# A decode layer on one core: K and V of the last heads in other pieces, one piece fewer of wo and of w2

## The chip, the core and the metric

The kernel runs on one core of a Trainium2 chip. TensorE (PE) multiplies matrices, with the loads of its weights shown apart (PEld); VectorE (DVE) and ScalarE (ACT) work on rows; GpSimd (POOL) fills and masks; SyncE (SP) issues most of the transfers from the chip's main memory, which run on 16 DMA engines. On-chip data lies in 128 partitions. The metric is the device time of one execution in microseconds; lower is better.

## The reference

One token passes through an attention block and a two-layer network, both conditioned on a vector c:

```python
mod = (_silu(c) @ w_mod).reshape(c.shape[0], 6, 1, -1)      # sa, ca, ga, sb, cb, gb
h = _layernorm(x) * (1 + ca) + sa
x = x + ga * _A_ref(h, k_cache, v_cache, wq, wo)            # attention, then @ wo
h = _layernorm(x) * (1 + cb) + sb
x = x + gb * (relu(h @ w1) @ w2)
```

x and c have 512 values. The attention has 32 query heads of 128 values and 8 heads of K and V; four query heads share one of these. K and V each hold 32,768 positions a head, so that each head has 8.4 MB of K and 8.4 MB of V, in bf16. wo is 4096 x 512 (4.2 MB), w1 512 x 1792 and w2 1792 x 512 (1.8 MB each). Nearly all of the data is K and V, and each byte is read once.

## The kernel before, in words

**Slots and stream.** All large data passes through three slots of 64 KB a partition (the pool `ring`). A slot holds all of one head's K, or its V, or w_mod with wq, or `tail_sb`: wo, w1 and w2. The slots are taken in turn, so K7 goes where V4 was, V6 where K6 was, V7 where V5 was, and the tail where K7 was; a transfer into a slot is issued when the last reader of its former content has finished. The list `stream` gives the order and the pieces of the transfers, and `load` issues them all from SP, which works through them in order: what waits at its head holds up all behind it. A key like `("k", 6, (0, 1))` is one transfer of tiles 0 and 1 of head 6; a head's K or V has four tiles of 64 positions a partition (2.1 MB each). Whoever needs one tile waits for the whole transfer that holds it. c and x are two small transfers issued from ACT, at the start.

**A head.** Each value of K must be transposed before TensorE can use it. `turn_k` does this on VectorE, in place (L441): a transpose a tile, or for the last head a transpose a half tile. `scores` (L460) multiplies the turned K with the queries, 16 products a tile. `softmax` takes the maximum, makes the exponentials P on ScalarE (L497) and transposes P on VectorE (L502). `pv` (L523) multiplies P with V, 16 products a tile. `blocks` and `o_cols` (L552 to L560) divide by the sum and place the head's output as columns of `oT_ps`; `normalise` (L574) and `spread` (L586, L590) bring the outputs of a group of heads, one group for each piece of wo, into the form that wo needs. The order of TensorE's and VectorE's instructions is written out by hand (`manual_schedule`): in a loop over heads, the scores of head g + 1 come before the products of head g with V. The heads from `HALVED` on (V of head 5, K of head 6) are loaded in halves, and the last two heads follow the loop in an order of their own.

**The end.** After the last products with V, `project` multiplies the heads' outputs with the pieces of wo. The first two pieces (six heads) go into rows (L599), which `join_rows` transposes and adds as columns (L617, L622); later pieces go into columns directly (L605), four small products for each of a head's four rows. `keep_clock` (L635) runs products whose result nobody uses. Then come x1T (L740), the second layernorm up to h2T (L307), the products with w1 (L765), relu (L775, L776), the products with w2 (L788: four for each of fourteen blocks, in the pieces of `W2P`), and the last sums (L793, L795).

Of the kernel before, what the change touches and what calls it, by code (L numbers as in the profile page):

```python
# [17 lines left out]
def kernel(  # L18
# [14 lines left out]
    nc = tc.nc  # L33
    P = 128
    _, _, D = A_x.shape
    _, Hkv, Sk, Dh = A_k_cache.shape
# [7 lines left out]
    NTILE = Sk // (P * TK)  # L44
    NG = NTILE // 2

    WOP = [(0, Hkv // 2), (Hkv // 2, Hkv // 4), (Hkv - 2, 1), (Hkv - 1, 1)]
    WOROWS = 2
    LAST = Hkv - 1
    LOOPED = Hkv - 2  # L50
    HALVED = LOOPED - 1
    W2P = [(0, 5), (5, 10), (10, 12), (12, 13), (13, 14)]
    W1P = [(0, KT)]

    OUT0, OUT1 = 30, 34
# [106 lines left out]
    whole, halves = [(0, 1, 2, 3)], [(0, 1), (2, 3)]  # L162
    stream = [("k", 0, halves[0]), ("wm",), ("wq",), ("k", 0, halves[1])]
    for g in range(LOOPED):
        stream += [("k", g + 1, s) for s in (halves if g >= HALVED else whole)] + [("v", g, s) for s in (halves if g >= HALVED else whole)]
    for s in halves:
        stream += [("k", LAST, s), ("v", LOOPED, s)]
    stream += [("v", LAST, (0, 1)), ("v", LAST, (2,)), ("v", LAST, (3,))] + [("wo", i) for i in range(len(WOP))]
    stream += [("w1", i) for i in range(len(W1P))] + [("w2", i) for i in range(len(W2P))]
    pos = [0]  # L170

# [8 lines left out]
    wm_sb = need(("wm",))  # L180
    cx_row = const.tile([16, D // 8], BF16)
    for i, row in enumerate((c[0], A_x[0, 0])):
        nc.scalar.dma_start(out=cx_row[8 * i:8 * i + 8], in_=row.rearrange("(a n) -> a n", a=8))

    ident_bf = const.tile([P, P], BF16)
    make_identity(nc, ident_bf[:])
# [372 lines left out]
    def o_cols(g):  # L559
        nc.tensor.matmul(  # L560
            oT_ps[:, REP * g:REP * (g + 1)], lhsT=Y_tiles.pop(g)[:], rhs=qsel,
            start=True, stop=True, skip_group_check=True,
        )
# [4 lines left out]
    def normalise(g):  # L568

        i = part_of(g)  # L570
        g0, n = WOP[i]
        CH = P // (n * REP)
        if g == g0 + n - 1:
            nc.vector.tensor_tensor(  # L574
                out=oA[i][:], in0=oT_ps[:, REP * g0:REP * (g0 + n)].unsqueeze(2).to_broadcast([P, n * REP, CH]),
                in1=cmask[n * REP][:].unsqueeze(1).to_broadcast([P, n * REP, CH]), op=ALU.mult,
            )
        PT_tiles.pop(g)
# [58 lines left out]
    with tc.manual_schedule(engines={mybir.EngineType.PE, mybir.EngineType.DVE}):  # L637
        build_qbd(0)
        for turn in (turn_k, scores):
            for u in range(NTILE):  # L640
                for half in range(2):
                    turn(0, u, half)
        open_o(0)
        for _ in softmax(0):
            pass
        soft = None
        for g in range(LOOPED):
            h = g + 1
            build_qbd(h)
            for u in range(NTILE):  # L650
                for half in range(2):
                    turn_k(h, u, half)
                    scores(h, u, half)
                if soft and u == 1:
                    next(soft, None)
            if g - 1 in [sum(w) for w in WOP]:
                spread(part_of(g - 2))
            if g >= HALVED:
                pv(g, (0, 1))
            soft = softmax(h)  # L660
            next(soft)
            if g > 0:
                blocks(g - 1)
            next(soft)
            if g > 0:
                o_cols(g - 1)
            next(soft)
            next(soft)
            pv(g, (2, 3) if g >= HALVED else (0, 1, 2, 3))
            if g > 0:  # L670
                normalise(g - 1)
            next(soft)
            open_o(h)
            next(soft)
        g, h = LOOPED, LAST
        build_qbd(h)
        turn_k(h, 0, 0)
        turn_k(h, 0, 1)
        next(soft, None)
        turn_k(h, 1, 0)  # L680
        turn_k(h, 1, 1)
        blocks(g - 1)
        scores(h, 0, 0)
        scores(h, 0, 1)
        scores(h, 1, 0)
        o_cols(g - 1)
        scores(h, 1, 1)
        normalise(g - 1)
        spread(part_of(g - 1))
        bank_max(h, 0)  # L690
        pv(g, (0, 1))
        for u in (2, 3):
            for half in range(2):
                turn_k(h, u, half)
                scores(h, u, half)
        bank_max(h, 1)
        soft = softmax(h)
        next(soft)
        next(soft)
        next(soft)  # L700
        pv(g, (2,), range(6))
        next(soft)
        next(soft)
        open_o(LAST)
        pv(g, (2,), range(6, 16))
        pv(g, (3,))
        next(soft)
        next(soft, None)
        end_b.append(two_banks("end_ps"))
        a_rows.append(row_bank(end_b[0][:, 0, :]))  # L710
        blocks(g)
        pv(LAST, (0, 1))
        o_cols(LAST - 1)
        normalise(LAST - 1)
        pv(LAST, (2,))
        spread(2)
        hid_ps = ps_o.tile([P, 512], F32, tag="o", name="hid_ps")
        nc.vector.memset(hid_ps[:], 0.0)
        pv(LAST, (3,))
        blocks(LAST)  # L720
        hid_st = piece("tail_sb", TAIL + 1280, 32 * FT + 2)
        nc.gpsimd.memset(hid_st, 0.0)
        project(0)
        keep_clock(2)
        o_cols(LAST)
        keep_clock(2)
        project(1)
        normalise(LAST)
        spread(3)
        keep_clock(2)  # L730
        project(2)
        keep_clock(1)
        join_rows()
        keep_clock(1)
        project(3)


        stat2 = const.tile([P, 2], F32)
        x1T = const.tile([P, KT], F32)
        nc.vector.tensor_tensor(out=x1T[:], in0=attnT_ps, in1=modT_sb[:, 2 * KT:3 * KT], op=ALU.mult)  # L740
        nc.vector.scalar_tensor_tensor(
            out=x1T[:], in0=x1T[:], scalar=1.0, in1=xT, op0=ALU.mult, op1=ALU.add, accum_out=stat2[:, 0:1],
        )
        h2T = const.tile([P, KT], BF16)
        x1_ps = []

        def meanwhile():
            e = expand(x1T[:], room("tail_sb", TAIL + 1024, [P, 32, KT]).rearrange("p (m kt) -> p m kt", kt=KT))
            keep_clock(2)
            x1_ps.append(four_rows(e, "x1"))  # L750
            keep_clock(2)

        keep_clock(3)
        layernorm_T(x1T[:], stat2, h2T[:], modT_sb[:, 3 * KT:4 * KT], ncb[:], "ln2", meanwhile)
        x1_rows = const.tile([OUT1, P], F32)
        nc.vector.tensor_copy(out=x1_rows[:], in_=x1_ps[0])
        ffn_ps = end_b[0][0:OUT1, 1, P:2 * P]
        nc.vector.memset(ffn_ps, 0.0)

        NQ = 32 * FT  # L760
        for part, (k0, k1) in enumerate(W1P):
            w1_sb = need(("w1", part))
            for kt in range(k0, k1):
                for q in range(4):
                    nc.tensor.matmul(  # L765
                        hid_ps[32 * q:32 * q + 1, 0:NQ], lhsT=h2T[:, kt:kt + 1],
                        rhs=w1_sb[:, kt - k0, q * NQ:(q + 1) * NQ], start=False, stop=(kt == KT - 1),
                        skip_group_check=True,
                    )
        keep_clock(3)  # L770
        hidT = room("tail_sb", TAIL, [P, 512])[:, 0:NQ].rearrange("p (f e) -> p f e", e=32)
        hid_v = hid_ps[:, 0:NQ].rearrange("p (e f) -> p f e", f=FT)
        hb = hid_st
        for f0, f1 in ((0, FT // 2), (FT // 2, FT)):
            nc.vector.transpose(out=hidT[:, f0:f1], in_=hid_v[:, f0:f1])  # L775
            nc.scalar.activation(  # L776
                out=AP(hb.tensor, hb.offset + 32 * f0 + 31, [hb.ap[0], [32, f1 - f0]]),
                in_=hidT[:, f0:f1, 0], func=ACT.Relu,
            )

        for part, (f0, f1) in enumerate(W2P):
            w2_sb = need(("w2", part))
            for ft in range(f0, f1):
                for i in (0, 2, 1, 3):
                    row = OUT0 + i
                    to, w = (0, 32) if row < 32 else (32, OUT1 - 32)
                    at = 32 * ft + 31 - (row - to)
                    nc.tensor.matmul(  # L788
                        ffn_ps[to:to + w, :], lhsT=hid_st[:, at:at + w], rhs=w2_sb[:, ft - f0, i * P:(i + 1) * P],
                        start=False, stop=(ft == FT - 1 and i % 2 == 1), skip_group_check=True,  # L790
                    )
        o_rows = const.tile([OUT1, P], F32)
        nc.vector.tensor_tensor(out=o_rows[:], in0=ffn_ps, in1=gb_rows[:], op=ALU.mult)  # L793
        o_bf = const.tile([OUT1, P], BF16)
        nc.vector.tensor_tensor(out=o_bf[:], in0=o_rows[:], in1=x1_rows[:], op=ALU.add)  # L795
# [31 lines left out]
```

## Time and profile before

| | us |
|---|---|
| median of 3 runs | 354.38 (354.29 to 354.51) |
| the profiled execution | 354.42 |
| its span, first to last instruction | 352.6 |
| PE busy | 272.3 (77%) |
| DVE busy | 195.6 (55%) |
| ACT busy | 18.7 (5%) |

The mean granted clock of TensorE was 0.926. The core read 149.42 MB from main memory.

In rows of the timeline the first number is the start in us from the start of the span, the second the busy time of the group in us; then engine, line of the code, operation, tiles written and read, shapes and count. In brackets stands how long the engine had been idle before it, and what ended that. An SPq row is the issue of a transfer, not the transfer itself. In rows of the chain of waits, start and duration are followed by what the chain went through. In rows of stretches, the stretch and its length are followed by the busy time and count of PE, PEld, DVE, ACT and POOL, the granted clock, the share of the transfers and GB/s.

### The profile page before, as it was taken

What the parts mean: (1) busy time and instruction counts of PE and PEld (TensorE: products, weight loads), DVE (VectorE), ACT (ScalarE), POOL (GpSimd) and SP (SyncE); (2) the same over time, 40 slices, a digit from 0 to 9 for tenths busy, and PEclk for the clock granted to TensorE, in tenths of its full rate; (3) what the DMA queues carried; (4) which work ended last, traced back from release to release, by engine and by line L of the source; (5) the groups of instructions that cost most, each with busy time, mean ns of one, the idle gap of its engine ahead of it and who ended that gap; (6) DMA issues with size and microseconds to landing.
All of it is one profiled execution on the core that took longest, in us unless ns stands there. A gap on an engine that the chain in (4) does not pass through costs nothing. (4 is left out here: it accounts for less than half of the span.)

```text
span 352.6 us, 3544 instructions
## 1 busy us (share of the span) xinstructions
PE 272.3 (77%) x1310; PEld 111.8 (32%) x1310; DVE 195.6 (55%) x167; ACT 18.7 (5%) x37; POOL 6.0 (2%) x26
## 2 busy tenths in 40 slices
PE   0054980695999679884988499976999999789994
PEld 0021330232333224331333233322444443234442
DVE  7662563983079513965099316956674293743142
ACT  1200003001000010001000100001000100011000
POOL 3000000000000000000000000000000000000000
PEclk9996895698999969998999979996999999999999
DMA  8999989999999999999999999999999999999995
GB/s 353 404 432 456 468 387 461 446 401 446 439 424 440 416 439 446 401 455 446 409 453 446 409 453 431 426 394 439 446 414 427 450 429 424 431 453 398 432 426 213
DMA packets 5222, 149.57 MB, mean 424 GB/s; under 512 B 604, under 2 KB 988, under 8 KB 1628
## 3 DMA queue, kind: packets, MB, share of 16 engines
q1 hardware_dynamic: 5180, 149.43, 98.5%
q8 instruction: 8, 0.13, 0.1%
q14 instruction: 2, 0.02, 0.0%
q10 hardware_dynamic: 32, 0.00, 0.0%
HBM read 149.42 MB, written 0.00 MB: 424 GB/s over the span
## 5 line engine op out<-in xcount | busy, mean ns | idle before, releaser
L441 DVE STREAM_TRANSPOSE Ksb<-Ksb 128x4096 f32<-128x4096 f32 (+1 forms) x34 | 131.5, 3912 | 57.6 <-DMA Ksb<-in_A_k_cache_dram 57.6
L460 PE MATMUL S_ps<-Ksb,qbd 128*128 128x512 bf16 x512 | 118.9, 385 | 19.2 <-DVE Ksb L441 18.3
L523 PE MATMUL o_ps<-Vsb,P_g 128*16 (+1 forms) x512 | 124.3, 401 | 10.9 <-ACT P_g L497 10.0
L460 PEld LDWEIGHTS <-qbd 128*128 128x128 bf16 x512 | 49.2, 97 | 84.9 <-issue 27.6
L523 PEld LDWEIGHTS o_ps<-Vsb,P_g 128*16 x320 | 30.4, 95 | 60.0 <-issue 31.8
L523 PEld LDWEIGHTS <-P_g 128*16 128x16 bf16 x192 | 16.7, 90 | 22.9 <-issue 0.4
L473 DVE TENSOR_REDUCE m_p<-S_ps 128x1 f32<-128x1024 f32 x7 | 8.6, 1223 | 21.8 <-PE S_ps L460 21.8
L502 DVE STREAM_TRANSPOSE P_g<-P_g 128x1024 bf16<-128x1024 bf16 x8 | 10.0, 1245 | 15.6 <-ACT P_g L497 15.6
L494 ACT ACTIVATE nbias<-Mb_ps 128x1 f32<-128x1 f32 x8 | 1.4, 171 | 269.5 <-PE Mb_ps L492 269.5
L324 PE MATMUL mod_ps<-wmq_sb,siluT 128*1 128x512 bf16 x24 | 3.6, 624 | 9.9 <-DMA wmq_sb<-in_w_mod_dram 9.9
L332 DVE STREAM_TRANSPOSE Ksb<-Ksb 128x4096 f32<-128x4096 f32 x2 | 8.8, 4424 | 1.7 <-DMA Ksb<-in_A_k_cache_dram 1.7
L478 PE MATMUL mT_ps<-ident_f,m_p 128*1 128x128 f32 x8 | 2.2, 270 | 8.9 <-DVE m_p L473 7.9
L497 ACT ACTIVATE P_g<-S_ps,nbias 128x1024 bf16<-128x1024 f32 x8 | 8.9, 1114 | 0.2
L560 PE MATMUL acc_ps<-mask_sb,Y 16*128 16x4 f32 x16 | 3.4, 282 | 5.1 <-DVE Y L556 5.1
L552 DVE SCALAR_TENSOR_TENSOR o_ps<-o_ps,Linv,smask 16x512 f32<-16x512 f32 x8 | 5.8, 720 | 2.8 <-PE o_ps L523 2.8
L254 PE MATMUL xc_ps<-cx_sel,wmq_sb 16*128 16x2 bf16 x4 | 0.3, 172 | 8.7 <-DVE wmq_sb L248 8.7
L590 DVE CAST o_sb<-o_ps 128x4 bf16<-128x4 f32 (+2 forms) x4 | 0.7, 167 | 11.1 <-PE o_ps L586 11.1
L415 POOL TENSOR_TENSOR qbd<-qrep_sb,rowpick 128x64 bf16<-128x64 bf16 x8 | 2.4, 299 | 228.0 <-PE S_ps L460 198.3
L509 DVE RECIPROCAL Linv<-L_ps 16x1 f32<-16x1 f32 x8 | 1.0, 126 | 8.3 <-PE L_ps L506 8.3
L556 DVE TENSOR_REDUCE Y<-o_ps 16x128 f32<-16x512 f32 x8 | 5.4, 679 | 0.3
L635 PE MATMUL spare_ps<-qbd,ident_bf 128*128 128x512 bf16 x18 | 5.4, 381 | 0.0
L396 PE MATMUL q_ps<-wmq_sb,hT 128*1 128x512 bf16 x32 | 3.6, 626 | 2.3 <-DMA wmq_sb<-in_A_wq_dram 2.3
(114 smaller groups left out, 71.6 us busy)
## 6 DMA issues: line engine op xcount, KB each, us to landing
Ksb<-in_A_k_cache_dram SPq DMA_DIRECT2D x5, 4096.0 KB, 22.9
Vsb<-in_A_v_cache_dram SPq DMA_DIRECT2D x5, 4096.0 KB, 36.5
wmq_sb<-in_A_wq_dram SPq DMA_DIRECT2D x1, 4096.0 KB, 28.1
Vsb<-in_A_v_cache_dram SPq DMA_DIRECT2D x2, 2048.0 KB, 41.1
Ksb<-in_A_k_cache_dram SPq DMA_DIRECT2D x1, 4032.0 KB, 37.2
wmq_sb<-in_w_mod_dram SPq DMA_DIRECT2D x1, 3072.0 KB, 18.9
tail_sb<-in_A_wo_dram SPq DMA_DIRECT2D x1, 2048.0 KB, 23.2
tail_sb<-in_B_w_dram SPq DMA_DIRECT2D x1, 1792.0 KB, 30.6
```

The costliest lines, as they stand in the source:

```text
L324: nc.tensor.matmul(dst[j // 4][32 * (j % 4):32 * (j % 4) + 1, :], lhsT=src_T[:, kt:kt + 1], rhs=w[:, kt, j * 512:(j + 1) * 512], start=(kt ...
L332: nc.vector.transpose(out=t, in_=t)
L396: nc.tensor.matmul(q_ps[i][32 * a:32 * a + 1, :].rearrange("o (h e) -> o h e", e=32), lhsT=hT[:, kt:kt + 1], rhs=wq_f[:, kt, i, a], start= ...
L441: t = nc.vector.transpose(out=KTt.bitcast(F32), in_=KTt.bitcast(F32))
L460: nc.tensor.matmul(S_ps_tiles[g], lhsT=qbd[g % 2][:, hp, 4 * (7 - s):4 * (7 - s) + P], rhs=KTv[:, 16 * sl:16 * sl + 16, h, :, par], start= ...
L473: behind_loop(nc.vector.reduce_max(out=m_p[:], in_=S_g.rearrange("p g f -> p (g f)"), axis=AX.X))
L497: nc.scalar.activation(out=P_g[:], in_=S_g.rearrange("p g f -> p (g f)"), func=ACT.Exp, bias=nbias[:], scale=scale, accum_out=l_g[:],)
L502: behind_loop(nc.vector.transpose(out=P_g[:], in_=P_g[:]))
L523: nc.tensor.matmul(o_tiles[g][:], lhsT=PT, rhs=Vx, start=first, stop=False, skip_group_check=True)
L552: nc.vector.scalar_tensor_tensor(out=o, in0=o, scalar=Linv_tiles.pop(g)[:], in1=smask[:].unsqueeze(2).to_broadcast([16, 4, Dh]), op0=ALU.m ...
L556: nc.vector.tensor_reduce(out=Y[:], in_=o.rearrange("p s d -> p d s"), op=ALU.add, axis=AX.X)
L635: nc.tensor.matmul(spare[0], lhsT=ident_bf[:], rhs=qbd[0][:, :, 0:P], start=True, stop=True)
```

## The change

- K of head 6 and V of head 5 are each loaded in one transfer instead of two halves.
- At the end of the stream the order was K7a, V6a, K7b, V6b, then V7's tiles 0 and 1, tile 2, tile 3. It is now K7a, K7b, V6a, V6b, V7a, V7b, all halves.
- K7's first half is turned inside the loop's last round, on VectorE ahead of the transpose of head 6's P. The scores of head 7 follow all together, and the products of P of head 6 with V6 come after them.
- wo has three pieces (heads 0 to 3, 4 and 5, 6 and 7) instead of four, so that the outputs of heads 6 and 7 are spread in one step after head 7. `join_rows` now stands ahead of the last piece, followed by six products of `keep_clock`.
- w2 has four pieces of 6, 5, 2 and 1 blocks instead of five of 5, 5, 2, 1 and 1.
- c is loaded in three transfers and x in four, instead of one each.

```diff
-    WOP = [(0, Hkv // 2), (Hkv // 2, Hkv // 4), (Hkv - 2, 1), (Hkv - 1, 1)]
+    WOP = [(0, Hkv // 2), (Hkv // 2, Hkv // 4), (Hkv - 2, 2)]
-    W2P = [(0, 5), (5, 10), (10, 12), (12, 13), (13, 14)]
+    W2P = [(0, 6), (6, 11), (11, 13), (13, 14)]
...
-        stream += [("k", g + 1, s) for s in (halves if g >= HALVED else whole)] + [("v", g, s) for s in (halves if g >= HALVED else whole)]
-    for s in halves:
-        stream += [("k", LAST, s), ("v", LOOPED, s)]
-    stream += [("v", LAST, (0, 1)), ("v", LAST, (2,)), ("v", LAST, (3,))] + [("wo", i) for i in range(len(WOP))]
+        stream += [("k", g + 1, whole[0]), ("v", g, whole[0])]
+    stream += [(x, g, s) for x, g in (("k", LAST), ("v", LOOPED), ("v", LAST)) for s in halves]
+    stream += [("wo", i) for i in range(len(WOP))]
...
-        nc.scalar.dma_start(out=cx_row[8 * i:8 * i + 8], in_=row.rearrange("(a n) -> a n", a=8))
+        for a, n in ((0, 2), (2, 2), (4, 2), (6, 2)) if i else ((0, 3), (3, 3), (6, 2)):
+            nc.scalar.dma_start(
+                out=cx_row[8 * i + a:8 * i + a + n], in_=row.rearrange("(a n) -> a n", a=8)[a:a + n],
+            )
...
+            if h == LOOPED:
+                build_qbd(LAST)
+                for u in (0, 1):
+                    for half in range(2):
+                        turn_k(LAST, u, half)
             next(soft)
             open_o(h)
             next(soft)
...
         o_cols(LAST - 1)
         normalise(LAST - 1)
         pv(LAST, (2,))
-        spread(2)
...
         project(1)
         normalise(LAST)
-        spread(3)
-        keep_clock(2)
+        spread(2)
+        join_rows()
+        keep_clock(6)
         project(2)
-        keep_clock(1)
-        join_rows()
-        keep_clock(1)
-        project(3)
```

Left out above is the written order of head 7's scores and of the products with V6, which is told in the list.

More of the change, by code (lines that the diff above doesn't have):

```diff
@@ L675 @@
         g, h = LOOPED, LAST
-        build_qbd(h)
-        turn_k(h, 0, 0)
-        turn_k(h, 0, 1)
         next(soft, None)
[L680 to L691, printed above, removed]
+        for u in (0, 1):
+            for half in range(2):
+                scores(h, u, half)
         for u in (2, 3):
@@ L695 @@
                 scores(h, u, half)
+        blocks(g - 1)
+        bank_max(h, 0)
         bank_max(h, 1)
@@ L699 @@
         next(soft)
+        o_cols(g - 1)
+        normalise(g - 1)
         next(soft)
-        pv(g, (2,), range(6))
+        spread(part_of(g - 1))
+        pv(g, (0,), range(6))
         next(soft)
@@ L704 @@
         open_o(LAST)
-        pv(g, (2,), range(6, 16))
-        pv(g, (3,))
+        pv(g, (0,), range(6, 16))
+        pv(g, (1,))
         next(soft)
@@ L710 @@
         a_rows.append(row_bank(end_b[0][:, 0, :]))
+        pv(g, (2, 3))
         blocks(g)
```

## The prediction

> **What bounds the kernel now.** I read the page first, its slices of the span and its chain of work, and then the chain of waits in order of time.
>
> ```profile
> DMA  8999989999999999999999999999999999999995
> HBM read 149.42 MB, written 0.00 MB: 424 GB/s over the span
> DMA 19%; PE 5%; DVE 3%; SPq 0%; issue 0%
> ```
>
> ```profile
> 313.20 25.28 DMA tail_sb<-in_A_wo_dram
> 338.50 11.12 DMA tail_sb<-in_B_w_dram
> 349.66 0.29 PE end_ps L788 x4
> ```
>
> The transfers are busy in every slice, and the chain that ends last is transfers from 313 to 349.6 us. The kernel is one uninterrupted stream of 149 MB at 424 GB/s; a half of a K or V (4.19 MB) takes 4.19/0.424 = 9.9 us of it. No byte is removed by the change. So it can move the time in three ways only: a hole in the stream, a cheaper stream, or work after the last bytes that no longer fits behind them. The third needs the timeline of the end, one row per group: start, duration, engine, line, and in brackets the idle time before it.
>
> ```profile
> 321.39 7.07 PE L523 MATMUL o_ps<-Vsb,P_g 128*16 128x512 bf16 x32
> 328.39 0.38 PE L560 MATMUL acc_ps<-mask_sb,Y 16*128 16x4 f32 x2
> 332.36 3.62 PE L523 MATMUL o_ps<-Vsb,P_g 128*16 128x512 bf16 x16
> 336.08 1.03 PE L599 MATMUL end_ps<-tail_sb,o_sb 128*1 128x512 bf16 x16
> 337.05 0.60 PE L635 MATMUL spare_ps<-qbd,ident_bf 128*128 128x512 bf16 x2
> 337.59 0.38 PE L560 MATMUL acc_ps<-mask_sb,Y 16*128 16x4 f32 x2
> 338.52 0.60 PE L599 MATMUL end_ps<-tail_sb,o_sb 128*1 128x512 bf16 x8
> 339.06 0.18 PE L586 MATMUL o_ps<-rsel,oA 128*128 128x4 bf16 x1
> 339.27 0.16 DVE L590 CAST o_sb<-o_ps 128x4 bf16<-128x4 f32 x1 [0.98 <-PE o_ps L586]
> 339.35 0.71 DVE L617 STREAM_TRANSPOSE tail_sb<-end_ps 128x512 f32<-128x512 f32 x1
> 340.60 0.24 PE L622 MATMUL acc_ps<-tail_sb,place 128*32 128x4 f32 x8
> 341.01 0.67 PE L605 MATMUL acc_ps<-o_sb,tail_sb 128*128 128x1 bf16 x16
> 341.71 0.16 DVE L740 TENSOR_TENSOR x1T<-acc_ps,modT_sb 128x4 f32<-128x4 f32 x1 [1.65 <-PE acc_ps L605]
> 343.74 0.22 DVE L307 SCALAR_TENSOR_TENSOR h2T<-cen_ln,rstd_ln,modT_sb 128x4 bf16<-128x4 f32 x1
> 345.33 0.93 PE L765 MATMUL hid_ps<-tail_sb,h2T 128*1 128x448 bf16 x16 [1.28 <-DMA tail_sb<-in_B_w_dram]
> 347.10 0.73 PE L788 MATMUL end_ps<-tail_sb 128*32 128x128 bf16 x20
> 348.30 1.64 PE L788 MATMUL end_ps<-tail_sb 128*32 128x128 bf16 x36 [0.47 <-DMA tail_sb<-in_B_w_dram]
> ```
>
> See two reserves here. h2T is ready at 343.74 + 0.22 = 343.96, but the w1 products start at 345.33, waiting for w1: 1.37 us. The w2 products run from 347.10 to 349.95, 2.85 us; at the pace of their first twenty (0.73 us) 56 would need about 1.75 us, so 1.1 us more is waiting for w2. Together about 2.45 us: a chain of engines that gets later by less costs nothing.
>
> The last V transfer, of one of V7's four tiles, was issued at 287.9 and landed 43.3 us later, at 331.2:
>
> ```profile
> L155 SPq DMA_DIRECT2D Vsb<-in_A_v_cache_dram x1: 433/433/433, 287.9 to 287.9; - x1
> DMA to landing us min/median/max: 43.3/43.3/43.3
> ```
>
> **The change, part by part.**
>
> *K6 and V5 whole; K7, V6, V7 in halves; K7's first half turned ahead of P of head 6.*
>
> ```profile
> 243.99 8.77 DVE L441 STREAM_TRANSPOSE Ksb<-Ksb 128x4096 f32<-128x4096 f32 x2 [1.86 <-DMA Ksb<-in_A_k_cache_dram]
> 257.61 0.33 SPq L155 DMA_DIRECT2D Ksb<-in_A_k_cache_dram  x1
> 257.91 14.08 PE L460 MATMUL S_ps<-Ksb,qbd 128*128 128x512 bf16 x64
> 258.09 8.74 DVE L441 STREAM_TRANSPOSE Ksb<-Ksb 128x4096 f32<-128x4096 f32 x2
> 301.96 8.89 DVE L441 STREAM_TRANSPOSE Ksb<-Ksb 128x2048 f32<-128x2048 f32 x4 [5.83 <-DMA Ksb<-in_A_k_cache_dram]
> 312.83 1.75 SPq L155 DMA_DIRECT2D tail_sb<-in_A_wo_dram  x4
> ```
>
> K6's first half lands at 243.99, so all of K6 9.9 us later, at about 253.8. Its four transposes (8.77 a pair) then end at 253.8 + 17.5 = 271.4 and the last quarter of scores at about 275, where before all scores ended at 257.91 + 14.08 = 272.0. So V6's first half, whose slot is K6's, is issued 3 us later. K7's two halves, now both issued when V4's slot comes free (257.61), lie ahead of it: 19.8 us of stream behind V5, which itself ends near 253.8 + 19.8 = 273.6. Covered by about 18 us. V5's products follow 3 us late and release V7's transfers near 290; the stream then holds K7's rest and V6, to about 311. Covered.
>
> K7's second half landed at 301.96 with V6's first half ahead of it; it now comes 9.9 us earlier, at 292. The turns of K7's first half, four at 2.2 us, hold up P of head 6 from 283 to 292; P is wanted only after the scores of head 7, so nothing waits. Those end near 292 + 1.3 (P's transpose) + 8.9 + 2 = 304.4 instead of 312.8, and wo's issue moves up as much. This gain is worth nothing: V7 fills the stream until 331 either way. Softmax 7 takes until about 307, V6's 64 products (2 x 7.07) until 321.4, and V7's first half runs from there to 328.9 with its small product (0.38), as before.
>
> *V7's second half in one piece.* Here the change costs. Before, tile 2 was multiplied while tile 3 was still coming, and after the last landing only one tile's sixteen products (3.62 us) were left: they ended at 332.36 + 3.62 = 335.98. Now 32 products (7.07 us) must wait for the last byte at 331.2, less a little for fewer pieces: I take 331.15, bounds 330.7 to 331.6. They end at 338.2. TensorE idles 2.3 us before them.
>
> *wo in three, one join later.* Everything from the end of V7's products, E, is one chain. The rows give: first product of wo at E + 0.10; o_cols at E + 1.61; second wo piece at E + 2.46 (it no longer waits for its bytes) to E + 3.06; spread 0.18 and cast 0.16 to E + 3.35; the transpose of the joined rows 0.71 to E + 4.07; the join 0.24, handing on at about E + 4.35; then keep_clock, now six products at 0.22 (two span 0.60, so 0.22 each after the first), which stand ahead of the last wo piece: 1.3, to E + 5.65; that piece, 32 small products where there were two times sixteen (0.67 each, 0.04 a product): 1.2, to E + 6.85. Before, the last piece's sixteen ended at E + 5.70 and were set by wo's landing. So x1T starts at 338.2 + 6.88 = 345.1 instead of 341.71: 3.4 us late, 2.2 from V7 and 1.2 from the order of wo.
>
> *w2 in four.* The last piece is the same fourteenth. h2T is ready at 343.96 + 3.4 = 347.35; w1 has long landed; w2 starts 1.77 later (347.10 - 345.33), at 349.15, with all of w2 there by 349.6, and runs unbroken: 1.75 us, to 350.9. Before it ended at 349.95. At the pace of the last 36 (1.64 us, waits included) 56 would take 2.55 and end at 351.7. I take the first pace, as those twenty waited for nothing.
>
> Sum: 3.4 late, 2.45 of reserve, **+0.95 us**; bounds +0.3 (landing at 330.7, quicker keep_clock) to +1.8. The profiled execution took 354.42 for its span of 352.6, the median is 354.38; I add 0.9 to that: **355.3 us**.
>
> *c and x in seven.* In the compiled program of the changed kernel the extra transfers use up the eight completion semaphores, so SP's w_mod now waits for c's first piece and wq for K0's first half.
>
> ```profile
> 7.99 0.68 DVE L248 TENSOR_TENSOR wmq_sb<-cx_row,pick 16x512 bf16<-16x512 bf16 x1 [1.50 <-DMA cx_row<-in_A_x_dram]
> 12.85 8.77 DVE L332 STREAM_TRANSPOSE Ksb<-Ksb 128x4096 f32<-128x4096 f32 x2 [1.71 <-DMA Ksb<-in_A_k_cache_dram]
> 60.27 13.10 DVE L441 STREAM_TRANSPOSE Ksb<-Ksb 128x4096 f32<-128x4096 f32 x3 [1.86 <-DMA Ksb<-in_A_k_cache_dram]
> 214.85 8.77 DVE L441 STREAM_TRANSPOSE Ksb<-Ksb 128x4096 f32<-128x4096 f32 x2 [10.74 <-DMA Ksb<-in_A_k_cache_dram]
> ```
>
> wq is issued when K0's half has landed, at 12.85; w_mod, 3.1 MB, keeps the stream full some 7 us more, and K0 is in the queue before c is asked for. I cost it at nothing in the stream. c and x themselves, two transfers of 1 KB, were usable at 7.99; seven may come at 8 or, queued one behind another, near 20. At 20 the two turns of K0's half (12.85, 8.77 us), which stand behind c and x on VectorE, and all that follows come 7 to 8 us late; K1's turns, which wait for bytes until 60.27 and have 1.86 us idle, come some 5 us late. By head 5 VectorE waits 10.74 us for K, so this is gone long before the end; without that cover it would be those 5 us.
>
> The Trainium skill (DMA: Bandwidth & Descriptors, on why a DMA increments its semaphore by 16) says that a transfer of two or three rows uses only the two or three lowest-numbered DMA engines; that would favour the late end, and no run so far shows it.
>
> **The rivals.**
>
> *The clock falls in the new gap.* Stretches with TensorE's busy time, and its granted clock third from the right:
>
> ```profile
> 300.60:304.00 3.40, 1.73 (x9) 0.64 (x7) 2.04 (x1) 0.00 (x0) 0.00 (x0) 1.00 1.05 453
> 235.80:239.20 3.40, 0.99 (x5) 0.58 (x4) 2.97 (x5) 0.00 (x0) 0.30 (x1) 0.93 1.03 443
> 239.20:242.60 3.40, 1.38 (x5) 0.57 (x5) 1.54 (x2) 1.38 (x3) 0.00 (x0) 0.50 1.03 443
> 290.00:313.00 23.00, 19.23 (x87) 7.79 (x84) 13.11 (x11) 0.00 (x0) 0.14 (x1) 1.00 1.00 432
> 338.00:349.00 11.00, 9.10 (x129) 4.38 (x129) 3.83 (x19) 0.76 (x3) 0.00 (x0) 1.00 0.97 401
> ```
>
> A stretch with 1.73 of 3.4 us busy kept the clock; one with 0.99 was followed by 0.50. The new gap of 2.3 us leaves 1.1 busy if it falls inside one such stretch, between the two. Half the clock for 3.4 us delays V7's products by 1.7 us: 357.0. The Trainium skill (TensorE: Matmul & The Clock Gate, Part 1) says that the clock is halved after an idle window of about 3.4 us, so 2.3 us would not do it; the row of 235.80 shows that a window need not be wholly idle.
>
> *The end stays with the transfers; faster.* Fewer, larger pieces: the last 11 us ran at 401 GB/s, the large pieces at 432. The 4.4 MB of those 11 us would take 10.2 at the better rate, 0.8 us less: 353.6. It decides only if the engine chain is late by less than 1.65 us at x1T, so that its 2.45 of reserve also covers those 0.8; I have 3.4, of which the seven microseconds of products behind V7's last landing are hard to argue away.
>
> *The parts cancel.* The chain comes out a microsecond shorter than summed, because its pieces overlap more, and the end is set by w2 again: 354.0 to 354.6.
>
> *A hole in the stream at the start*, if w_mod's issue waits for a c that comes late: K0's first half is all there is until about 13, so c at 16 would cost 3 us: 358.
>
> **How the numbers follow.** My forecast 0.55, the clock 0.16, cancelling 0.13, the hole and other stalls 0.07, faster 0.09. A difference of 0.2% (0.7 us) is about what this kernel's measurement tells from none. Of my forecast, +0.3 to +1.8, some 0.4 of the 0.55 lies above 0.7 us: slower 0.63, same 0.28, faster 0.09. The range 354.2 to 357.2 leaves out the faster case and the hole; the forecast's own is 354.7 to 356.2.
>
> **What would show it.** Right: TensorE idle about 2 us until V7's second half lands near 331; 32 products to 338; x1T near 345; w1 and w2 products without waiting for transfers, and the chain of work's last 10 us on engines. Wrong: x1T before 343.5, idle before w2, a clock of 0.5 after 328, or a slice of the transfers under 8 near the start.

## The result and the profile after

| | before | after |
|---|---|---|
| median, run side by side on one chip (22 runs each) | 354.25 us | 354.98 us |
| ratio, 95% interval | | 1.0028 (1.0022 to 1.0034) |
| the profiled execution, its span | 354.42, 352.6 us | 354.87, 353.0 us |
| start of o_rows, the first of the last two sums | 349.98 us | 350.30 us |
| V7's last transfer there for TensorE | 331.2 us | 330.67 us |

The change makes the kernel 0.73 us slower. Single executions, of the kernel before too, now and then took 361 us and more; these are left out everywhere below.

The page of the profile after: TensorE's and VectorE's busy time, the slices of the transfers, the packets, and the chain's shares. Ahead of it stands the one line of the page before that the prediction did not show.

```profile
DMA packets 5222, 149.57 MB, mean 424 GB/s; under 512 B 604, under 2 KB 988, under 8 KB 1628
```

```profile
PE 274.6 (78%) x1311; PEld 113.0 (32%) x1311; DVE 194.0 (55%) x163; ACT 18.7 (5%) x37; POOL 5.8 (2%) x25
...
DMA  8999989999999999999999999999999999999994
...
DMA packets 4501, 149.57 MB, mean 424 GB/s; under 512 B 524, under 2 KB 780, under 8 KB 1164
...
DMA 26%; PE 6%; DVE 5%; issue 0%; ACT 0%; DVEq 0%
```

The transfers are still busy in every slice: no hole. There are 721 packets fewer for the same bytes. The last slice is a 4 where it was a 5: the last packets of the stream end at 348.75, where they ended at 349.30 before, and yet the span is longer. So the work behind the last bytes has become the longer part. The timeline of the end shows it (start, busy time, engine, line, and in brackets the idle time before):

```profile
315.13 13.97 PE L525 MATMUL o_ps<-Vsb,P_g 128*16 128x512 bf16 x64
...
329.04 0.38 PE L562 MATMUL acc_ps<-mask_sb,Y 16*128 16x4 f32 x2
...
330.67 6.63 PE L525 MATMUL o_ps<-Vsb,P_g 128*16 128x512 bf16 x30 [1.26 <-DMA Vsb<-in_A_v_cache_dram]
...
337.36 0.38 PE L525 MATMUL o_ps<-Vsb,P_g 128*16 128x512 bf16 x1
...
341.91 1.47 PE L637 MATMUL spare_ps<-qbd,ident_bf 128*128 128x512 bf16 x6
...
343.22 1.20 PE L607 MATMUL acc_ps<-o_sb,tail_sb 128*128 128x1 bf16 x32
...
344.46 0.16 DVE L737 TENSOR_TENSOR x1T<-acc_ps,modT_sb 128x4 f32<-128x4 f32 x1 [2.78 <-PE acc_ps L607]
...
346.47 0.22 DVE L309 SCALAR_TENSOR_TENSOR h2T<-cen_ln,rstd_ln,modT_sb 128x4 bf16<-128x4 f32 x1
...
346.75 0.93 PE L762 MATMUL hid_ps<-tail_sb,h2T 128*1 128x448 bf16 x16
...
348.51 1.74 PE L785 MATMUL end_ps<-tail_sb 128*32 128x128 bf16 x56
...
350.30 0.28 DVE L790 TENSOR_TENSOR o_rows<-end_ps,gb_rows 34x128 f32<-34x128 f32 x1 [1.86 <-PE end_ps L785]
...
350.93 0.29 SPq L793 DMA_DIRECT2D out_dram<-o_bf  x1
```

TensorE waits 1.26 us for V7's last half, multiplies until 337.74, and from there everything follows without a wait for a transfer: the products with w1 start 0.06 after h2T, and the 56 products with w2 run unbroken. From the landing to o_rows it takes 19.63 us. What the prediction named as its signs is there, but the wait for V7, named as about 2 us, is shorter: V7 landed 0.5 earlier than forecast, and the products before it ended 0.5 later (329.41 against 328.9), because the clock was halved behind the last softmax. Neither changes the mechanism.

One line needs care. The chain of waits of after ends as follows (start, duration, what it went through):

```profile
289.69 31.26 DMA Vsb<-in_A_v_cache_dram
...
320.97 27.27 DMA tail_sb<-in_B_w_dram
348.24 0.23 ACT tail_sb L773
...
348.51 1.76 PE end_ps L785 x54
```

Read literally, relu (L773) was held by a transfer that landed at 348.24, and the end still belongs to the stream. But relu reads no weights; it reads what VectorE transposes. In all the profiles of this document it starts 0.5 after the first of the two transposes does (348.23 after 347.73 here), whichever releaser the view names, and in the kernel e8 below the chain passes through VectorE. So it is the transpose that sets it, and a piece of `tail_sb` landed at the same moment.

The middle went as laid out. From the timeline after: K6's four turns, the scores' last quarter, V6's and V7's issues, K7's first half turned, wo's issue.

```profile
253.44 8.77 DVE L443 STREAM_TRANSPOSE Ksb<-Ksb 128x4096 f32<-128x4096 f32 x2 [11.48 <-DMA Ksb<-in_A_k_cache_dram]
...
270.97 3.64 PE L462 MATMUL S_ps<-Ksb,qbd 128*128 128x512 bf16 x16 [0.69 <-DVE Ksb L443]
...
274.64 15.85 SPq L155 DMA_DIRECT2D Vsb<-in_A_v_cache_dram  x4
...
282.32 8.89 DVE L443 STREAM_TRANSPOSE Ksb<-Ksb 128x2048 f32<-128x2048 f32 x4
...
303.73 1.28 SPq L155 DMA_DIRECT2D tail_sb<-in_A_wo_dram  x3
```

And the start, with c and x in seven transfers: first use of c and x, K0's turns, the issues of V0 and of V2.

```profile
17.30 0.68 DVE L250 TENSOR_TENSOR wmq_sb<-cx_row,pick 16x512 bf16<-16x512 bf16 x1 [11.30 <-DMA cx_row<-in_A_x_dram]
...
21.75 8.75 DVE L334 STREAM_TRANSPOSE Ksb<-Ksb 128x4096 f32<-128x4096 f32 x2
...
39.16 0.35 SPq L155 DMA_DIRECT2D Vsb<-in_A_v_cache_dram  x1
...
120.12 0.33 SPq L155 DMA_DIRECT2D Vsb<-in_A_v_cache_dram  x1
```

c and x are usable 9.3 us later than before (7.99), V0 is issued 3.8 us later (39.16 against 35.36), V2 at 120.12 against 120.07: the delay has run out.

### The profile page after: what moved, and what is told of

Read it like the earlier page. It is cut to its first block, busy times and chain, and to the rows that moved or that the text cites. A ratio compares the mean times of both kernels' runs of the same rounds, so it can differ in the third digit from the quotient of the medians.

```text
span 353.0 us, 3546 instructions
## 1 busy us (share of the span) xinstructions
PE 274.6 (78%) x1311; PEld 113.0 (32%) x1311; DVE 194.0 (55%) x163; ACT 18.7 (5%) x37; POOL 5.8 (2%) x25
## 5 line engine op out<-in xcount | busy, mean ns | idle before, releaser
L525 PE MATMUL o_ps<-Vsb,P_g 128*16 (+1 forms) x512 | 126.5, 409 | 11.8 <-ACT P_g L499 10.0
L347 PE MATMUL t_ps<-ident_f,wmq_sb 128*128 128x128 f32 x8 | 1.9, 372 | 6.4 <-DVE modT_sb L348 5.7
L483 DVE TENSOR_REDUCE Mrow<-mT_ps 1x4 f32<-1x128 f32 x8 | 2.2, 273 | 5.2 <-PE mT_ps L480 5.2
```

The lines of the kernel that those rows point to most:

```text
L525: nc.tensor.matmul(o_tiles[g][:], lhsT=PT, rhs=Vx, start=first, stop=False, skip_group_check=True)
```

## The experiments

The theory is one sentence: o_rows starts at the later of two times, that of the stream (the last bytes of w2 and the few products behind them, near 349.5 to 350) and that of the engines (V7's last landing plus a chain of fixed length). Two parts of the change lengthen the chain, V7's halves and wo's order; neither alone should show. The rivals: that c and x cost the time at the start; that the clock costs it in the new gap; that w2 still sets the end.

This table collects all profiles, in us. "V7" is the start of the products that wait for V7's last piece, where they do; "end" is the span less the start of the output's issue; the median is that of the timed runs, beside the kernel before on the same chip.

| kernel | V7 | x1T | o_rows | end | median | before |
|---|---|---|---|---|---|---|
| before | | 341.71 | 349.98 | 2.0 | 354.25 | |
| after | 330.67 | 344.46 | 350.30 | 2.1 | 354.98 | 354.25 |
| e1 after, V7 in tiles | | 343.13 | 349.50 | 2.5 | 354.60 | 354.28 |
| e2 after, no keep_clock(6) | 330.78 | 343.28 | 349.49 | 2.1 | 355.69 | 354.28 |
| e3 after, gap filled | 330.90 | 344.69 | 350.54 | 2.0 | 355.10 | 354.28 |
| e11 after, softmax gap filled | 331.33 | 345.11 | 350.96 | 2.0 | 356.62 | 354.28 |
| e4 after, c and x in two | 330.95 | 344.74 | 350.59 | 2.4 | 355.52 | 354.33 |
| e5 before, V7 in halves | 330.87 | 343.49 | 349.64 | 2.5 | 354.59 | 354.33 |
| e6 before, wo in three | | 342.50 | 349.58 | 2.5 | 354.65 | 354.33 |
| e8 before, both | 331.04 | 344.82 | 350.67 | 2.7 | 355.70 | 354.33 |
| f1 e1 with SPACE 13 | | 342.43 | 349.51 | 2.3 | 354.30 | 354.28 |
| f2 e4 with SPACE 19 | 331.10 | 344.89 | 350.74 | 2.8 | 355.85 | 354.28 |
| f3 before with SPACE 13 | | 341.43 | 349.69 | 2.1 | 354.22 | 354.28 |
| f4 e11 once more | 330.96 | 344.75 | 350.60 | 2.0 | 355.13 | 354.28 |

**V7's halves and wo's order, each alone and both, on the kernel before (e5, e6, e8).** The edits; e8 has both. In e5 and e8 keep_clock(8) fills the new gap, so that the clock is no part of the answer.

```diff
-    stream += [("v", LAST, (0, 1)), ("v", LAST, (2,)), ("v", LAST, (3,))] + [...]
+    stream += [("v", LAST, s) for s in halves] + [...]
...
         normalise(LAST - 1)
+        keep_clock(8)
         pv(LAST, (2,))
```

```diff
-    WOP = [(0, Hkv // 2), (Hkv // 2, Hkv // 4), (Hkv - 2, 1), (Hkv - 1, 1)]
+    WOP = [(0, Hkv // 2), (Hkv // 2, Hkv // 4), (Hkv - 2, 2)]
...
-        spread(2)
...
-        spread(3)
-        keep_clock(2)
-        project(2)
-        keep_clock(1)
+        spread(2)
         join_rows()
-        keep_clock(1)
-        project(3)
+        keep_clock(6)
+        project(2)
```

> The kernel before, with V7 in two halves, and eight products of keep_clock in the gap ahead of the second, so that the clock plays no part. My theory: V7's products end 2.2 us later, at 338.2, and x1T comes 2.2 us later, near 343.9; this is less than the reserve of 2.45 us, so the time does not change: 354.2 to 354.5. A rival in which each part of the change costs in proportion (no reserve): some two thirds of the change's 0.7 us, 354.8.

> The kernel before, with wo in three pieces and join_rows and six products of keep_clock ahead of the last. My theory: V7's products end at 336.0 as before, x1T comes 6.7 us later, at 342.7, 1.0 us late and within the reserve: no change, 354.1 to 354.4. In proportion: 354.6.

> The kernel before with both: V7 in two halves, eight products of keep_clock in the gap, and wo in three with its order. My theory: 338.1 + 6.7 = 344.8 at x1T, 3.1 us late, 0.65 over the reserve: 354.9, though each of the two alone costs nothing; o_rows starts near 350.6. If the order in the middle or the start made the loss, this has neither and stays at 354.3.

Timeline of the end of e5, then of e6, then of e8:

```profile
330.87 3.61 PE L523 MATMUL o_ps<-Vsb,P_g 128*16 128x512 bf16 x16 [0.36 <-DMA Vsb<-in_A_v_cache_dram]
...
343.49 0.16 DVE L741 TENSOR_TENSOR x1T<-acc_ps,modT_sb 128x4 f32<-128x4 f32 x1 [1.41 <-PE acc_ps L605]
...
347.56 2.04 PE L789 MATMUL end_ps<-tail_sb 128*32 128x128 bf16 x56
```

```profile
342.50 0.16 DVE L736 TENSOR_TENSOR x1T<-acc_ps,modT_sb 128x4 f32<-128x4 f32 x1 [2.77 <-PE acc_ps L605]
...
346.71 0.73 PE L784 MATMUL end_ps<-tail_sb 128*32 128x128 bf16 x20
...
347.98 1.56 PE L784 MATMUL end_ps<-tail_sb 128*32 128x128 bf16 x36 [0.54 <-DMA tail_sb<-in_B_w_dram]
```

```profile
331.04 6.63 PE L523 MATMUL o_ps<-Vsb,P_g 128*16 128x512 bf16 x30 [0.46 <-DMA Vsb<-in_A_v_cache_dram]
...
344.82 0.16 DVE L737 TENSOR_TENSOR x1T<-acc_ps,modT_sb 128x4 f32<-128x4 f32 x1 [2.78 <-PE acc_ps L605]
...
348.89 1.74 PE L785 MATMUL end_ps<-tail_sb 128*32 128x128 bf16 x56
```

Against x1T at 341.71 before, V7's halves alone make it 1.78 late, wo's order alone 0.79 (its V7 products ended 0.47 earlier than before, so the order itself costs 1.26), both together 3.11. The first two leave o_rows below 349.98: in e6 TensorE still waits 0.54 for w2; in e5 the 56 products take 2.04 where unbroken ones take 1.74. With both, o_rows moves to 350.67, 5.85 behind x1T. In after, e3, e4, f2 and f4 the distance is 5.84 or 5.85 too. So x1T may come as late as some 343.65 (349.5 - 5.85) for nothing; after is 0.8 beyond that. For o_rows, two parts that are harmless alone are not harmless together.

The chain of waits of e8 shows relu released by VectorE:

```profile
348.10 0.43 DVE tail_sb L772
...
348.60 0.24 ACT tail_sb L773
...
348.89 1.76 PE end_ps L785 x54
```

The medians alone would not have told this. Those of e5 and e6 are 0.3 above the kernel before though their o_rows is not later, and for e6 that is just what the rival in proportion asked (354.6); of the 1.37 that e8 is above, only 0.69 lies in o_rows. The rest is the column "end", and not the theory's; it comes last. What tells the theory from that rival is the wait for w2, still there in e5 and e6 and gone in e8.

**V7's pieces undone in the changed kernel (e1).**

```diff
-    stream += [(x, g, s) for x, g in (("k", LAST), ("v", LOOPED), ("v", LAST)) for s in halves]
+    stream += [(x, g, s) for x, g in (("k", LAST), ("v", LOOPED)) for s in halves]
+    stream += [("v", LAST, (0, 1)), ("v", LAST, (2,)), ("v", LAST, (3,))]
```

> The changed kernel, with V7 again in three transfers (tiles 0 and 1, tile 2, tile 3). My theory (the end is the later of the stream of transfers and the chain of engines behind V7's last landing): V7's products no longer wait for a whole half and end near 336.4 instead of 337.74, the chain is 1.3 us earlier, and the end falls back on the last bytes of w2, 0.85 us sooner: 354.1 us. A rival in which the loss comes from the start (c and x) or from the order in the middle: no change, 354.9.

The products with w2 wait for bytes again (timeline of e1):

```profile
347.19 0.84 PE L786 MATMUL end_ps<-tail_sb 128*32 128x128 bf16 x24
...
348.21 1.25 PE L786 MATMUL end_ps<-tail_sb 128*32 128x128 bf16 x32 [0.17 <-DMA tail_sb<-in_B_w_dram]
...
349.50 0.28 DVE L791 TENSOR_TENSOR o_rows<-end_ps,gb_rows 34x128 f32<-34x128 f32 x1 [2.37 <-PE end_ps L786]
```

o_rows is 0.80 earlier than in after, as the theory asks, and the median falls from 0.73 above the kernel before to 0.3 above it (1.0011, 1.0001 to 1.002). That it does not fall to 354.1 lies in the end, 2.5 instead of 2.1.

**keep_clock(6) left out (e2).** The six idle products stand ahead of the last piece of wo.

```diff
         join_rows()
-        keep_clock(6)
         project(2)
```

> The changed kernel without the six products of keep_clock ahead of the last piece of wo. My theory: the same chain is 1.3 us shorter at another place, with V7 left as it is; the end again falls on the last bytes of w2, so the gain is the same 0.85 us and no more: 354.1 us. A rival in which V7's wait alone matters: no change, 354.9. If the clock drops for want of these products, 355 or more.

The profiled execution, 354.07, did what the theory says: x1T at 343.28 though V7 landed as late as in after, w2 waiting for bytes, o_rows at 349.49. The other four took 355.17 to 356.52, none of them profiled. So the six products cost 1.3 us of chain (from V7 to x1T 12.50 where after has 13.79), and without them something dearer comes in most runs. That it is the clock is not shown.

**The new gap filled (e3), and the softmax gap filled (e11, f4).** This is about the scatter, not about the 0.73 of the medians. After's own runs scatter upward: 15 of 22 at 354.80 to 355.05, 7 from 355.39 to 356.80, where the kernel before stays within 0.5. The clock rival says that these are runs in which the gap of 1.26 us before V7's last half halved the clock. From 250 us on, the profile after shows one halved stretch, behind the last softmax, harmless since it lies over V6's products that have time to spare. The last row holds the gap before V7's last half:

```profile
304.05:307.45 3.40, 1.80 (x10) 0.92 (x10) 1.89 (x7) 0.00 (x0) 0.18 (x1) 1.00 1.05 453
307.45:310.85 3.40, 3.40 (x10) 1.11 (x9) 1.19 (x1) 2.58 (x4) 0.00 (x0) 0.50 0.98 424
...
327.90:331.30 3.40, 2.14 (x11) 0.97 (x10) 0.00 (x0) 0.00 (x0) 0.00 (x0) 1.00 0.87 371
```

e3 puts five idle products into V7's gap, e11 (and f4, the same kernel) eight into the softmax gap:

```diff
         normalise(LAST - 1)
+        keep_clock(5)
         pv(LAST, (2,))
```

```diff
         soft = softmax(h)
+        keep_clock(5)
         next(soft)
         next(soft)
         o_cols(g - 1)
+        keep_clock(3)
```

> The changed kernel with five products of keep_clock in TensorE's gap before V7's second half (329.4 to 330.7). Theory of the clock in this gap: the changed kernel's scatter upward (355.4 to 356.8 in 7 of 22 runs) comes from half clock after this gap; with it filled all runs lie within 354.8 to 355.1. My rival: the gap is too short to matter and the scatter stays, with about a third of the runs above 355.3.

> The changed kernel with five and three products of keep_clock in TensorE's gaps around the softmax of head 7 (303.9 to 306.3), after which the profile shows half clock for 3.4 us. Theory: a longer fall of the clock from here delays the products of V6 and V7 beyond the 1.3 us of idle time left before V7's second half, and this makes the runs of 355.4 to 356.8; with the gaps filled they vanish and the idle time before V7's second half grows to about 2.5 us. If the scatter has another source it stays.

> The kernel with keep_clock(5) behind the last softmax and keep_clock(3) behind its o_cols once more, for its profile, since its time has come out in two groups, 355.0 to 355.5 and 356.6 to 356.9. Theory that the second group is the gap before the last half of V of head 7 (2.31 long in its first profile) followed by a halved clock: if the profile is of that group, a stretch behind 333 shows the clock near 0.5 for some 3.4, and the last 32 products of L525 end 1.7 later than 6.6 behind the landing. Rival: the 1.7 lies elsewhere, the clock behind the gap is 1.0 and the products take 6.6. If the profile is of the first group it tells neither.

e3: 354.89 to 355.50 in nine runs. Its theory asked for all of them within 354.8 to 355.1, and four lie above; its rival asked for a third above 355.3, and two do. None is above 355.5, where after had 5 of 22, but at that rate nine runs without one would come about one time in ten ((17/22) to the ninth). So e3 settles nothing. e11 went the other way than its theory: the clock behind the softmax was whole, as it also is in e3 and f1, which leave that gap as it was, yet three of five runs took 356.62 to 356.92. The wait for V7 had grown: without the slow stretch the products before it ended 0.4 sooner (329.02 against 329.41), and V7 landed later. Timeline of e11, then of f4, and a stretch of e11 with its gap:

```profile
331.33 6.63 PE L525 MATMUL o_ps<-Vsb,P_g 128*16 128x512 bf16 x30 [2.31 <-DMA Vsb<-in_A_v_cache_dram]
...
350.96 0.28 DVE L792 TENSOR_TENSOR o_rows<-end_ps,gb_rows 34x128 f32<-34x128 f32 x1 [1.86 <-PE end_ps L787]
```

```profile
330.96 6.63 PE L525 MATMUL o_ps<-Vsb,P_g 128*16 128x512 bf16 x30 [2.13 <-DMA Vsb<-in_A_v_cache_dram]
...
350.60 0.28 DVE L792 TENSOR_TENSOR o_rows<-end_ps,gb_rows 34x128 f32<-34x128 f32 x1 [1.86 <-PE end_ps L787]
```

```profile
327.90:331.30 3.40, 1.12 (x6) 0.56 (x5) 0.00 (x0) 0.00 (x0) 0.00 (x0) 1.00 0.98 419
331.30:334.70 3.40, 3.37 (x16) 1.43 (x16) 0.00 (x0) 0.00 (x0) 0.00 (x0) 1.00 1.02 436
```

Here a stretch with only 1.12 us busy was followed by the full clock, while the one of after with 1.80 was followed by half. The place of the stretch explains this. In every trace the halved stretches last 3.41 us or a multiple of it and start multiples of 3.41 apart, on a grid that lies differently in each execution (one starts at 307.47 in after, at 306.13 in e4). Over the stretches of this grid, in the 14 traces and from 50 us on, each one at full clock in which TensorE was busy for under 1.58 us was followed by half the clock, none with over 1.93 was, and between the two both happen. The stretch of e11 just shown lies across the grid; the two on the grid that share its gap have 2.83 and 1.68.

By this, a gap of 2.3 halves the clock in those executions in which it falls into one stretch of the grid. Both profiles of this kernel are of others: they fell on short runs (355.49 and 355.13), with products at full pace. That fits e11's long runs, which are 1.1 to 1.9 us longer than its short ones, around the 1.7 that the prediction worked out for half the clock over one stretch. It does not explain after's or e2's: the gaps of their profiles leave at least 2.16 and 2.08 busy in any 3.41 us around them, so the long runs would need a longer gap than was profiled. The mean granted clock, on record for every run, does not sort long from short: the longest runs of e4 and f2 have 0.938, their profiled ones 0.923. No profile shows a halved clock in V7's gap; this stays open.

**c and x undone (e4).**

```diff
-        for a, n in ((0, 2), (2, 2), (4, 2), (6, 2)) if i else ((0, 3), (3, 3), (6, 2)):
-            nc.scalar.dma_start(
-                out=cx_row[8 * i + a:8 * i + a + n], in_=row.rearrange("(a n) -> a n", a=8)[a:a + n],
-            )
+        nc.scalar.dma_start(out=cx_row[8 * i:8 * i + 8], in_=row.rearrange("(a n) -> a n", a=8))
```

> The changed kernel with c and x in one transfer each, as before. My theory: the start is hidden; c and x are usable at 8.0 instead of 17.3 us and V0 is issued near 35.4 instead of 39.2, and nothing else changes: 354.9 in the runs at full clock, with single runs up to 356.8. A rival that puts the loss at the start: 354.2.

c and x are usable at 7.93 again, and nothing is won: 355.52. That c and x cost the time at the start is refuted. The kernel is even 0.5 above after: 0.3 is a later landing of V7 (330.95 against 330.67), the rest the end.

**The end behind the output's issue (f1, f2, f3).** In e1, e4, e5, e6 and e8 the span goes on 2.4 to 2.7 us after the output is issued, in before, after, e2, e3 and e11 2.0 or 2.1. The timeline lists no engine's work there. In the second group SP and ACT have together 149 instructions in the compiled program, in the first 144, 147, 148 or 150. So I formed a theory that the place of the last instructions in the program decides, and moved it by SPACE, the number of idle drains that SP runs once V of head 0 is issued: 13 in f1 (e1 otherwise) and f3 (before otherwise), 19 in f2 (e4 otherwise).

```diff
-    SPACE = 14
+    SPACE = 13
```

> The changed kernel with V of head 7 in tiles 0 and 1, 2, 3 (as in the run before it of this kind), and SPACE, the number of idle drains on SP after V of head 0, 13 instead of 14: one instruction less on SP, long before the end. Theory that where the last instructions lie in the program decides how long the end takes: the output's issue stays near 350.1 and the span ends 2.0 to 2.1 behind it instead of 2.5, so 354.1 to 354.2. Rival, that the end's length belongs to the pieces of V and not to the place: 2.5 stays, 354.6.

> The changed kernel with c and x in one transfer each, and SPACE 19 instead of 14, so that SP and ACT have together as many instructions as in the changed kernel. Theory that c and x are worth nothing beside the place of the last instructions: the end behind the output's issue goes from 2.4 to 2.0 or 2.1, and the time to that of the changed kernel, 354.9 to 355.1. Rival, that c and x in seven transfers themselves save the 0.4 (the gap before the last half of V was 1.62 with two, 1.26 with seven): 355.4 stays.

> The kernel before with SPACE 13 instead of 14 and nothing else. Theory that the place of the last instructions decides the end's length: the output's issue stays at 350.6 and the span ends 2.5 behind it instead of 2.0, so 354.7. Rival, that one idle instruction more or less changes nothing: 354.3.

The count of instructions falls: f2 has 149 and the longest end of all, 2.8; f3 has 148 and keeps 2.1 and the time of before (1.0000, 0.999 to 1.001). Only f1 moved as expected, and half as far: 2.3, 354.30 instead of 354.60. The end is steady within a kernel (e8's five runs lie within 0.16 us). What sets it is in the traces, in SP's waits at the program's last line. Here is SP's wait for the output's transfer (us in total, times, longest) in after, e5, e8, f1 and f2, which have ends of 2.1, 2.5, 2.7, 2.3 and 2.8:

```profile
SPq L819 <- DMA out_dram<-o_bf: 0.5, 1, 0.5
```

```profile
SPq L823 <- DMA out_dram<-o_bf: 0.6, 1, 0.6
```

```profile
SPq L819 <- DMA out_dram<-o_bf: 0.7, 1, 0.7
```

```profile
SPq L820 <- DMA out_dram<-o_bf: 0.8, 1, 0.8
```

```profile
SPq L816 <- DMA out_dram<-o_bf: 0.9, 1, 0.9
```

The output has landed 1.2 us after its issue in all 14 traces. But SP meets its wait for it sooner or later: it goes through the eight semaphores of the transfers in one fixed order, and the transfers use these in turn, so the number of transfers in the program decides how many waits still stand behind the output's.

| kernels | transfers | waits behind the output's | pause behind it | end |
|---|---|---|---|---|
| before, after, e2, e3, e11, f3, f4 | 40 | 0 | no | 2.0 to 2.1 |
| e5, e6 | 39 | 1 | yes | 2.5 |
| e8 | 38 | 2 | yes | 2.7 |
| f1 | 41 | 4 | no | 2.3 |
| e1 | 41 | 4 | yes | 2.5 |
| e4 | 35 | 5 | no | 2.4 |
| f2 | 35 | 5 | yes | 2.8 |

A wait behind it takes 0.06 to 0.1. The pause is one of 0.45 between two of SP's last instructions, which stood still for nothing that the trace names; it moves with SPACE (e1 and f1, e4 and f2; in e1 only 0.2 of it shows), and in before it lies ahead of the landing, where it costs nothing, as its absence in f3 shows. What the pause is stays open. So the place decides about the pause, and the rest of the end goes with the number of transfers. f1 is the best form of the changed kernel that I found, and equal to the kernel before: 1.0007 (0.9996 to 1.0017). Nothing here beats it.

## Why the prediction was right, and where its terms were off

The forecast was 355.3, with a range of 354.2 to 357.2 and most of the chance on slower by over 0.2%; the median is 354.98, slower by 0.28%. The mechanism is the one forecast, and e8, e1 and the pair e5 and e6 show it in x1T and o_rows by adding and removing its two halves. That the medians differ by 0.73, so near the 0.95 of the forecast, is in part luck: the landing and the chain came out 0.64 earlier than summed, and the profile from which the sum starts was itself 0.3 late.

- *V7's last half lands at 331.15, bounds 330.7 to 331.6.* This term was mis-sized by 0.5: 330.67 in the profile after, a hair outside the bounds. In the eight other profiles with V7 in the same two halves the products start at 330.78 to 331.33, all but one before 331.15, and f4 lies 0.37 before e11, which is the same code. The weak step is the one from a single profile: its landing is one draw of a time that moves by some 0.4 from run to run. That fewer pieces made it earlier is not shown: e5 and e8, with the other pieces of K and V as before, have 330.87 and 331.04.
- *Products of 7.07, then 6.88 to x1T.* Measured 7.07 (330.67 to 337.74) and 6.72. The chain, worked out piece by piece from the rows, was good to 0.16; wo's share of it, put at 1.2, is 1.0 in after (6.72 - 5.73) and 1.26 in e6.
- *Reserve of 2.45.* e5 (1.78 late) and e6 (0.79 late) lie below it and did not move o_rows; e8 (3.11 late) moved it by 0.69 where 3.11 - 2.45 gives 0.66. Right.
- *w2's products unbroken in 1.75.* 1.74, and 1.76 after w1's start where 1.77 was taken. Right.
- *The sum.* +0.95 forecast; between the two profiled executions +0.45. The landing (0.48) and the chain (0.16) together make 0.64 less at x1T; o_rows came at 350.30, and w2's products had been forecast to end at 350.9; the end of the span added 0.1. Between the medians it is +0.73: f3, the kernel before but for one drain, has o_rows at 349.69, so the profile of before, 354.42 where the median is 354.25, was itself a late one; against f3's, o_rows of after is 0.61 late.
- *The middle costs nothing.* K6 forecast to land at 253.8, measured 253.44; scores to end near 275, V6 issued at 274.64; V7 issued near 290, its two issues ending the group at 290.5; wo's issue 304.4, measured 303.73, a gain worth nothing. Right. e1 and f1, which have all of the change but V7's pieces, confirm it.
- *c and x cost nothing in the stream, usable at 8 to 20.* 17.3, 3.8 us late at V0 and gone by V2, earlier than the head 5 that was named. The Trainium skill's rule (DMA: Bandwidth & Descriptors, on why a DMA increments its semaphore by 16) that such transfers use few engines spoke for the late end; the trace agrees with the direction, and does not show which engines carried them.
- *The rival of the faster stream.* It had two halves. That the stream got cheaper is not shown: where it sets the end, o_rows is at 349.49 to 349.51 with after's pieces (e1, e2, f1) against 349.58 to 349.98 with those of before (e6, f3, before), but the last packets of the stream end at 348.75 to 349.42 in the nine profiles with after's pieces and at 348.94 to 349.30 in the five others. The 0.8 of the rival is not there. And x1T was 2.75 late, more than the 1.65 up to which the rival would have decided.
- *The rival of the clock.* It was given 0.16 as the outcome of the median. It did not decide the median, but something of its size strikes part of the runs. The reading behind it, that a stretch with 1.73 us busy keeps the clock and one with 0.99 does not, was too simple: its stretches did not lie on the clock's grid, and on the grid the border is between 1.58 and 1.93 us busy.

## What to carry to other kernels

In a kernel that is one stream of transfers, split or join pieces by one question: how much work can only start with the last byte of this piece, and what reserve does the chain behind it have? Work out the reserve from the idle times before the last consumers, and add up the delays of all parts before comparing them with it: two parts that cost nothing alone can cost 0.7 us together. Where a few tenths of a microsecond are at stake, compare the start of the last useful instruction across kernels, and not only their medians, and look at what SP still waits for behind the output's issue.

## What the runs showed of the hardware that was not expected

- The end of the program, from the output's issue to the end of the span, took 2.0 to 2.8 us though the output had always landed after 1.2. What made the difference was the number of waits that stood behind the output's (0 with 40 transfers, 5 with 35) and a pause of 0.45 that moved when one idle instruction, 300 us earlier, was left out.
- The clock halves by a grid of 3.41 us, which lies differently in each execution. On it, under 1.58 us of work in a stretch was always followed by half the clock, over 1.93 never. The Trainium skill (TensorE: Matmul & The Clock Gate, Part 1) names an idle window of about 3.4 us; here the measurement decides, and a window that was half busy was enough (1.80 of 3.40 us in after).
- c and x in seven transfers of 0.2 to 0.4 KB were usable 9.4 us later than in two of 1 KB (17.30 against 7.93 in e4), with the stream of large transfers running beside them.
- A kernel's transfers land up to 0.4 us apart from run to run at the same place of the stream (V7 in e11 and f4), though the medians of the kernel before on four occasions, 354.25 to 354.33, agree to 0.1.
